# Holding back two groups of loads beside DMA transposes in the first phase of a fused attention and expert kernel

## The chip, the cores and the metric

The kernel runs on one core of one Trainium2 chip. The metric is the device time of one execution in microseconds (us); a lower time is better. The engines are named PE (matrix multiply; PEld in the tables is its loading of weights), DVE (vector), ACT (scalar), POOL (which here mostly issues loads) and SP (which here issues the DMA transposes). Times within a trace are counted from the start of the span, which reaches from the first to the last instruction.

## The reference, cut to what matters

Eight batches of linear attention with eight heads are computed, and their output goes through eight experts with a balanced (Sinkhorn) gate. Only the attention and the first expert matter here.

```python
def phi(x, c, s):                       # cos and sin weights of the position
    r = np.maximum(x, 0.0)
    return np.concatenate([r * c, r * s], axis=-1)
q_p = phi(q, cos_w, sin_w)
k_p = phi(k, cos_w, sin_w)
kv = np.einsum('bhsf,bhsd->bhfd', k_p, v)
z = np.sum(k_p, axis=2)
num = np.einsum('bhsf,bhfd->bhsd', q_p, kv)
den = np.einsum('bhsf,bhf->bhs', q_p, z)[..., None] + 1e-06
# num / den is x of the experts: out += P[:, e] * (relu(x @ w1[e]) @ w2[e])
```

## The kernel before

The first phase runs in blocks. Block j does the first expert on 512 tokens in 16 slots, eight of the first matrix product (`ffn1`, PSUM tile `h_ps`, result `hT`) and eight of the second (`ffn2`, `y_ps`). Between the slots stands the attention work of other batches: in block 1, the third batch (number 2 in the code) is finished and the fourth (number 3) is prepared. In the code, `hk` counts the four pairs of heads; `zsel` holds the sums of the scaled keys, `rb` the reciprocals of the denominators, and `xT` is x, the input of the experts. In the traces an instruction that waits holds up those written behind it on its engine: before the change the value copy at 55.41 us on DVE, whose v had landed by 43.19, ran only after a `q_p` that had waited 7.94 us.

Loads go through POOL's software queue into four buffers for each of q, k and v; a load takes half a batch. The scaled queries `q_p` of batch 2 and later are turned by a DMA transpose that SP issues; there are three `q_p` buffers, and one comes free when its transpose has landed (in the trace before, the first transpose landed at 53.97 us, and the `q_p` that waited for its buffer began at 54.07).

```python
ld = p1.enter_context(tc.tile_pool(name="ld", bufs=4))
qp_pool = p1.enter_context(tc.tile_pool(name="qp_pool", bufs=3))
rb_pool = p1.enter_context(tc.tile_pool(name="rb_pool", bufs=4))
# ...
def load(b, half, names="qkv", held_back=False):
    for name in names:
        x = ld.tile([P, 2, C, D], F16, name=f"{name}_ld")
        # ... i = nc.gpsimd.dma_start(out=x, in_=this half of the batch)
        if held_back:
            after(ve.last, i)          # wait for DVE's last instruction so far

def prep_q(b, hk):
    q16 = loaded.pop(("q", b, hk))
    # ... from batch 2 on: relu in place on DVE
    q_p = qp_pool.tile([P, C, 2, D], F16, name="q_p")
    ve.tensor_tensor(out=q_p[:], in0=q16.unsqueeze(2).to_broadcast([P, C, 2, D]),
                     in1=cs, op=ALU.mult)
    # ... from batch 2 on:
    nc.sync.dma_start(out=qTs[b, hk], in_=q_p[:].rearrange("p c a d -> p (c a d)"),
                      transpose=True)
```

The schedule of block 1 (j = 1, b = 2), cut:

```python
# the third batch (b): its scaled keys and values, sums, denominators, x
for hk in range(HK):
    if hk >= 2:
        at(j, 0, prep_k, b, hk, False)
    at(j, 0, prep_kp, b, hk)
    at(j, (0, 0, 1, 3)[hk], prep_v, b, hk, (ve.tensor_copy, se.copy)[hk // 2])
at(j, 3, sums, b, 0)                 # PE; afterwards zsel on DVE
at(j, 5, sums, b, 1)
at(j, 6, denominators, b)            # PE needs zsel and the four transposed q
for hk in range(HK):
    at(j, (9, 10, 12, 13)[hk], attend, b, hk)      # PE, then xT on DVE
# the fourth batch (b + 1)
    (4, prep_q, 0), (5, prep_q, 1), (6, prep_k, 0), (7, prep_q, 2),
    (8, prep_k, 1), (9, prep_q, 3), (10, prep_kv, 0), (10, prep_k, 2),
    (12, prep_kv, 1), (12, prep_k, 3), (13, prep_kv, 2), (14, prep_kv, 3),
# block 2 begins on the fifth batch with (3, prep_k, 0) on ACT
```

The softmax here doesn't subtract the row's maximum and nothing guards it: scores larger than these inputs give would overflow.

## Time and profile before

| | before |
|---|---|
| median of the first 3 runs | 989.77 us (989.68 to 989.98) |
| PE busy over the span | 969.5 of 988.3 us |
| PE idle in one piece, 48.97 to 55.91 us | 6.94 us |
| PE's clock at half | 53.96 to 60.79 us |

The page's own lines on busy time (first) and on the chain of work that ended last (second) say that PE bounds the kernel, so a microsecond that counts is one in which PE stands or runs slower.

```profile
PE 969.5 (98%) x7877; PEld 676.3 (68%) x7877; DVE 807.0 (82%) x1833; ACT 565.3 (57%) x1263; POOL 60.6 (6%) x82
...
PE 93%; DVE 2%; ACT 2%; DMA 2%; POOL 0%; issue 0%; ACTq 0%; SPq 0%; DVEq 0%; POOLq 0%
```

The table of 10 us stretches shows, for each, PE's busy time (with the number of its instructions), the same of the other engines, then PE's clock, the DMA share and GB/s. One row differs from the rest.

```profile
core 0: us, PE busy (x) PEld busy (x) DVE busy (x) ACT busy (x) POOL busy (x), PEclk, DMA share, GB/s
40.00:50.00 10.00, 8.97 (x53) 4.06 (x51) 5.37 (x13) 7.93 (x18) 0.86 (x2) 1.00 1.20 201
50.00:60.00 10.00, 3.74 (x42) 2.02 (x43) 5.83 (x13) 1.13 (x4) 0.00 (x0) 0.70 0.83 132
60.00:70.00 10.00, 10.00 (x123) 5.00 (x122) 7.19 (x17) 6.21 (x16) 0.00 (x0) 0.96 0.51 86
```

PE's timeline about the hole. In square brackets stand the idle time before the instruction and what ended it.

```profile
45.32 3.66 PE L109 MATMUL h_ps<-xT,w1e 128*128 128x512 f16 x16
55.91 0.68 PE L109 MATMUL small_ps<-acc_lo,k_p 64*128 64x65 f16 x18 [6.94 <-DVE acc_lo L109]
56.94 0.68 PE L109 MATMUL small_ps<-acc_lo,k_p 64*128 64x65 f16 x18 [0.35 <-DVE acc_lo L109]
57.55 3.48 PE L109 MATMUL h_ps<-xT,w1e 128*128 128x512 f16 x8
60.96 0.75 PE L109 MATMUL small_ps<-acc_lo,k_p 64*128 64x65 f16 x36
```

PE waits 6.94 us for `acc_lo`, which is where the third batch's value copies lie. The line at 57.55 shows the second loss: eight matmuls of 512 columns take 3.48 us. DVE's timeline says why the copies are late.

```profile
45.83 0.30 DVE L109 TENSOR_SCALAR q_ld<-q_ld 128x576 f16<-128x576 f16 x1
54.07 0.76 DVE L109 TENSOR_TENSOR q_p<-q_ld,acc_hi 128x1152 f16<-128x1152 f16 x1 [7.94 <-DMA q_pT<-q_p]
54.74 0.75 DVE L109 TENSOR_TENSOR k_p<-k_ld,acc_hi 128x1152 f16<-128x1152 f16 x1
55.41 0.44 DVE L109 COPY acc_lo<-v_ld 128x576 f16<-128x576 f16 x1
```

DVE has a `q_p` to write and no buffer for it until the first transpose has landed. In the chain of waits, that transpose is one piece.

```profile
39.69 14.29 DMA q_pT<-q_p
...
54.07 0.76 DVE q_p L109
```

The transpose takes 14.29 us from issue to landing; transposes that are issued alone later land after 3.2 to 3.6 us. What stands beside it is in POOL's timeline: the six loads of the fourth batch, issued as soon as buffers are free. (The last line shown is the first load of the fifth batch.)

```profile
33.86 0.72 POOL L201 DMA_DIRECT2D k_ld<-in_k_dram  x1 [0.61 <-DMA w2e<-in_moe_w_dram]
...
40.84 0.72 POOL L201 DMA_DIRECT2D v_ld<-in_v_dram  x1 [0.70 <-ACT rb L109]
71.58 0.72 POOL L201 DMA_DIRECT2D q_ld<-in_q_dram  x1 [30.02 <-DVE acc_lo L109]
```

In the trace these six land between 45.16 and 53.96 us, one each 1.3 to 2 us.

### The profile page before, as it was taken

To read this page: it belongs to the slowest core of one execution; us is meant where nothing else is said; L and a number is where in the kernel's file an instruction comes from. 1 tells how busy PE (TensorE), PEld (TensorE's weight loads), DVE (VectorE), ACT (ScalarE), POOL (GpSimd) and SP (SyncE) were. 2 spreads that over 40 slices of the span, in tenths; PEclk is the share of its full clock that TensorE was granted. 3 is DMA by queue.
4 is the path that set the end of the run, shared out by engine and by line. 5 is a ranking of instruction groups with operands and counts; after the bars stand their busy time and mean duration, and the time that the engine had idled before them with its cause. 6 is when DMAs were issued, how large, how long until landed. Compare 5 with 4: busy or idle time off the path is not lost.

```text
span 988.3 us, 20283 instructions
## 1 busy us (share of the span) xinstructions
PE 969.5 (98%) x7877; PEld 676.3 (68%) x7877; DVE 807.0 (82%) x1833; ACT 565.3 (57%) x1263; POOL 60.6 (6%) x82
## 2 busy tenths in 40 slices
PE   9979999989999999999999999999999999999997
PEld 6535544447777777777777777777777777777775
DVE  6666774779889888988789888988789888988887
ACT  5746665467776555555555555555555555555551
POOL 6312110010000000000000000000000000000001
PEclk9989999999999999999999999999999999999999
DMA  9968991633013310133113410133103400104535
GB/s 162 204 111 147 162 148 31 126 62 73 26 48 68 69 47 25 34 83 68 41 33 67 85 31 26 49 67 68 49 25 67 92 25 26 48 26 113 132 86 128
DMA packets 80336, 73.54 MB, mean 74 GB/s; under 512 B 33264, under 2 KB 72176, under 8 KB 80240
## 3 DMA queue, kind: packets, MB, share of 16 engines
q0 software_dynamic: 27232, 30.94, 20.0%
q1 hardware_dynamic: 52768, 41.06, 16.9%
q8 instruction: 61, 1.00, 0.4%
q14 instruction: 35, 0.29, 0.1%
q10 hardware_dynamic: 240, 0.26, 0.1%
HBM read 83.12 MB, written 12.98 MB: 97 GB/s over the span
## 4 chain that ended last, share of the span: by engine, by line
PE 93%; DVE 2%; ACT 2%; DMA 2%; POOL 0%; issue 0%; ACTq 0%; SPq 0%; DVEq 0%; POOLq 0%
PE rows_ps L109 34%; PE h_ps L109 27%; PE copied_ps L109 11%; PE p_ps L109 11%; PE y_ps L109 6%; PE small_ps L109 4%; DMA q_pT<-q_p 1%; ACT hT L109 0%; DVE acc_hi L913 0%; POOL hs_last L928 0%; DVE P_tok L109 0%; DMA out_dram<-acc_lo 0%; DVE colp L109 0%; ACT u L109 0%; ACT acc_lo L109 0%
## 5 line engine op out<-in xcount | busy, mean ns | idle before, releaser
L913 DVE SCALAR_TENSOR_TENSOR acc_lo<-rows_ps,P_tok,acc_lo 128x512 f32<-128x512 f32 (+1 forms) x322 | 203.5, 641 | 74.7 <-PE rows_ps L109 74.6
L109 PEld LDWEIGHTS <-H 128*128 128x128 f16 x2080 | 203.0, 98 | 83.1 <-issue 1.2
L849 ACT CAST u<-h_ps 128x384 f16<-128x384 f32 x288 | 137.8, 478 | 131.2 <-PE h_ps L109 131.2
L109 PEld LDWEIGHTS <-w1e 128*128 128x128 f16 x1632 | 156.8, 98 | 67.5 <-issue 8.0
L843 DVE CUSTOM_DVE_ANT_0 H<-p_ps,u 128x384 f16<-128x384 f32 x329 | 181.4, 551 | 6.5 <-PE p_ps L109 6.4
L109 PEld LDWEIGHTS <-hs 128*128 128x128 f16 x1500 | 146.6, 98 | 56.2
L109 PE MATMUL h_ps<-S,w1e 128*128 128x384 f16 x672 | 164.1, 326 | 1.1 <-ACT u L109 0.9
L109 PE MATMUL p_ps<-xT,T 128*128 128x384 f16 x672 | 164.1, 326 | 0.1
L109 PE MATMUL h_ps<-xT,w1e 128*128 128x384 f16 (+1 forms) x616 | 151.6, 354 | 0.2 <-DVE xT L109 0.2
L109 PE MATMUL rows_ps<-V,H 128*128 128x256 f16 x1000 | 150.0, 273 | 0.7 <-DVE acc_hi L913 0.7
L109 PE MATMUL rows_ps<-w2e,hs 128*128 128x256 f16 x1000 | 150.0, 273 | 0.0
L881 ACT ACTIVATE H<-h_ps 128x384 f16<-128x384 f32 x144 | 70.7, 491 | 95.0 <-PE h_ps L109 95.0
L109 PEld LDWEIGHTS <-T 128*128 128x128 f16 x1008 | 98.1, 98 | 29.2 <-issue 2.8
L109 PE MATMUL rows_ps<-w2e,H 128*128 128x256 f16 (+1 forms) x568 | 91.2, 285 | 0.0
L862 ACT COPY copied_ps<-h_ps 128x384 f32<-128x384 f32 x144 | 67.5, 469 | 35.2 <-PE h_ps L109 35.2
L872 ACT ACTIVATE H<-copied_ps 128x384 f16<-128x384 f32 x144 | 70.9, 492 | 20.3 <-PE copied_ps L109 20.3
L109 PE MATMUL copied_ps<-xT,w1e 128*128 128x384 f16 x336 | 82.1, 326 | 0.0
L109 PE MATMUL h_ps<-S,T 128*128 128x384 f16 x336 | 81.8, 325 | 0.3 <-ACT copied_ps L109 0.3
L109 PE MATMUL copied_ps<-w2e,H 128*128 128x256 f16 x504 | 75.5, 272 | 0.0
L109 PE MATMUL rows_ps<-V,hs 128*128 128x256 f16 x500 | 75.0, 272 | 0.0
L913 DVE SCALAR_TENSOR_TENSOR acc_lo<-copied_ps,P_tok,acc_lo 128x256 f32<-128x256 f32 x126 | 60.2, 478 | 0.4
L913 DVE SCALAR_TENSOR_TENSOR acc_hi<-rows_ps,P_tok,acc_hi 128x512 f32<-128x512 f32 (+1 forms) x56 | 41.3, 738 | 20.5 <-PE rows_ps L109 19.7
(147 smaller groups left out, 953.5 us busy)
## 6 DMA issues: line engine op xcount, KB each, us to landing
S<-x_saved SPq DMA_DIRECT2D x108, 192.0 KB, 2.4
out_dram<-acc_lo SPq DMA_DIRECT2D x62, 128.0 KB, 2.4
w1e<-in_moe_w_dram POOLq DMA_DIRECT2D x7, 1024.0 KB, 9.0
w2e<-in_moe_w_dram POOLq DMA_DIRECT2D x7, 1024.0 KB, 9.7
q_ld<-in_q_dram POOLq DMA_DIRECT2D x16, 288.0 KB, 7.4
k_ld<-in_k_dram POOLq DMA_DIRECT2D x16, 288.0 KB, 8.2
v_ld<-in_v_dram POOLq DMA_DIRECT2D x16, 288.0 KB, 9.6
x_saved<-S SPq DMA_DIRECT2D x18, 192.0 KB, 1.9
```

What stands on the lines that cost most here:

```text
L109: i = getattr(self.engine, name)(*args, **kwargs)
L843: latest = ve._custom_dve(TENSOR_ADD_SAT, out=out, in0=ps[:, 0:TU], in1=t[:], s0=FP32_MAX, s1=0.0)
L849: se.copy(out=t[:], in_=ps[:, 0:TU])
L862: se.copy(out=Y[:, 0:TU], in_=X[:, 0:TU])
L872: se.activation(out=h11, in_=Y[:, 0:TU], func=AF.Relu)
L881: se.activation(out=h12, in_=X[:, 0:TU], func=AF.Relu)
L913: ve.scalar_tensor_tensor(out=a, in0=rows, scalar=P_tok[:, g, self.e : self.e + 1], in1=a, op0=ALU.mult, op1=ALU.add,)
```

## The change

The intent is to let the third batch's transposes pass before the fourth batch's loads, and then the fourth batch's transposes before the fifth batch's loads. Nothing else moves: set against each other, the two kernels have the same instructions in the same order on PE, DVE, ACT and SP. On POOL the fourth batch's loads also change their order from k, k, q, q, v, v to q, k, v for each half.

```diff
@@ block 1, after the third batch's second prep_v @@
+                        if hk == 1:
+                            for half in range(2):
+                                at(j, 0, load, b + 1, half, "qkv", True)
@@ the loads of the batch after next @@
-            if j == 0:
+            if j and b + 2 < B:
                 for half in range(2):
-                    at(1, 0, load, b + 2, half)
-            elif b + 2 < B:
-                for half in range(2):
-                    at(j, 11 + half, load, b + 2, half, "qkv", True)
+                    at(j, (14 if j == 1 else 11) + half, load, b + 2, half, "qkv", True)
```

## The prediction

> **What bounds the kernel.** The page gives PE 969.5 of 988.3 us (98%); the chain that ended last is 93% PE. The change touches only the first 100 us. There the table of 10 us windows shows one hole: PE is busy 3.74 of 10 us in 50-60, mean clock 0.70. The timeline shows PE idle 6.94 us before 55.91, waiting for the third batch's value copies on DVE; DVE sat idle 7.94 us before 54.07, until a DMA transpose q_pT<-q_p landed (it frees one of three q_p buffers). The chain of waits holds it as one DMA item of 14.29 us from 39.69; transposes issued later, alone, land in 3.2 to 3.5 us. Reason: six loads of the fourth batch are issued at 33.9 to 40.8, and the software queue moves about 205 GB/s; the last lands at 53.96. From 44 to 51 both queues get the same packet rate. [...] After the hole PE runs at half clock: eight 512-column matmuls take 3.48 us, elsewhere about 1.73. The hole costs 6.9 + about 1 (second copy) + 1.7, about 9.6 us.
>
> **What the change does.** PE, DVE, ACT and SP instructions and their order are the same; 12 loads on POOL move. The fourth batch's six now wait for the copy of the third batch's second values (about 49.1 us) instead of free buffers, and go q,k,v per half. The fifth batch's wait for DVE's last value copy (76.2 before) instead of 71.3. No bytes change.
>
> **Gain.** The first transpose no longer competes: estimate, landing near 46 instead of 54. The copies are then ready at 48 and 49, just when PE needs them (49.0). Hole and half clock vanish: -9.6 us.
>
> **Given back (estimates from the trace's landing times).** With a quiet queue six loads issued from t land at t+4.4, +6, +7.5, +9, +10.5, +12.
> 1. The fourth batch's first q, issued at 49.4, lands near 53.8. DVE, in order, has its relu and q_p before the third batch's second zsel, which PE wants in slot 6 at 53.5: PE waits about 1.7 us.
> 2. The fourth batch's transposes (from 55) now collide with these loads, which end near 61.5; the last q_p needs the first transpose's buffer near 61.4 and gets it near 63. The x products behind it on DVE come late: about 1.5 us of PE in slots 12 and 13.
> 3. The fifth batch's first k lands about 6 us after 70.8, near 77; ACT wants it in slot 3 of block 2, near 74.5. ACT is blocked with two h_ps buffers: about 1.5 us of PE; the second half's k another 0.5.
> Together about 5 of the 9.6 us. [...] After block 2 all only shifts.
>
> **Prediction.** 985.2 us, 8 in 10 within 982.3 to 988.0. Chances: faster by over 2% 0.01, within 2% 0.98, slower by over 2% 0.01.
>
> **What would show it.** The DVE wait for q_pT<-q_p shrinks from 7.9 to under 3 us and moves to about 61; clock 1.0 through 50-60; a new DVE wait for q_ld of 2 to 4 us near 50-54; PE gaps near 54 (behind zsel), 63 (behind xT) and 77 (behind hT); ACT waits for k_ld in block 2; phases after 100 us of equal length.
>
> **What would make it wrong.** If the transposes at 55 to 62 suffer like the one at 39.69, the hole returns smaller in block 1: 988 or more. If the late loads land a little earlier than counted, slack hides items 2 and 3: 981 to 983.

Its landing times for a quiet queue are estimates from the trace before, where six loads issued from 112.35 us landed 4.39, 6.77, 8.18, 9.61, 11.10 and 12.50 us after that, and six issued from 131.99 us 4.75, 6.17, 7.65, 9.08, 10.51 and 12.14 us after that.

## The result, and the profile after

| | before | after |
|---|---|---|
| median | 989.88 us (989.68 to 990.12, 4 runs) | 987.47 us (986.80 to 988.09, 4 runs) |
| ratio to before | | 0.9976, 95% interval 0.9958 to 0.9993 |

A ratio is the mean time of one kernel's runs over that of the other's runs of the same rounds, so it is not quite the ratio of the medians. The gain is 2.4 us by the medians, where the hole and its half clock had cost about 9.6 us by the prediction's count. The question is where the rest went. To see it, the span is cut at four PE instructions that both kernels have. A is the first matmul of block 1, B the first of the third batch's `attend` (slot 9 of block 1), C the first of block 2, D the first of block 3. The columns are differences of their start times.

| us | up to A | A to B | B to C | C to D | D to the end | span |
|---|---|---|---|---|---|---|
| before | 45.32 | 21.22 | 8.84 | 19.65 | 893.25 | 988.28 |
| after | 45.68 | 13.01 | 11.56 | 22.83 | 893.30 | 986.38 |
| difference | +0.36 | -8.21 | +2.72 | +3.18 | +0.05 | -1.90 |

So 8.2 us were won in the first part of block 1, and 5.9 us were given back, in the rest of block 1 and in block 2. From block 3 on nothing changed. The stretches of the profile after:

```profile
40.00:50.00 10.00, 10.00 (x94) 4.93 (x91) 8.80 (x20) 7.93 (x19) 0.35 (x1) 1.00 0.86 146
50.00:60.00 10.00, 9.01 (x116) 4.40 (x115) 6.93 (x17) 6.44 (x15) 3.93 (x6) 1.00 1.02 157
60.00:70.00 10.00, 7.80 (x70) 3.90 (x69) 7.03 (x17) 4.76 (x11) 0.00 (x0) 1.00 0.86 143
70.00:80.00 10.00, 7.81 (x123) 4.21 (x116) 6.28 (x15) 4.91 (x12) 4.28 (x6) 1.00 0.77 115
80.00:90.00 10.00, 9.24 (x58) 4.44 (x57) 6.94 (x15) 6.91 (x17) 0.00 (x0) 1.00 1.22 174
```

The hole in 50-60 and its clock of 0.70 are gone, but PE's busy time is now short by 2.2 us in 60-70 and again in 70-80. PE's timeline after names the waits; the second line answers to the one at 55.91 before.

```profile
45.68 3.66 PE L109 MATMUL h_ps<-xT,w1e 128*128 128x512 f16 x16
49.27 0.74 PE L109 MATMUL small_ps<-acc_lo,k_p 64*128 64x65 f16 x36
49.95 1.90 PE L109 MATMUL h_ps<-xT,w1e 128*128 128x512 f16 x8
51.78 0.75 PE L109 MATMUL small_ps<-acc_lo,k_p 64*128 64x65 f16 x36
...
55.16 0.56 PE L109 MATMUL small_ps<-q_pT,zsel 128*32 128x192 f16 x12 [0.72 <-DVE zsel L109]
...
65.52 0.54 PE L109 MATMUL small_ps<-q_pT,kv_sb 128*64 128x384 f16 x4 [2.06 <-DVE xT L109]
...
79.84 1.02 PE L109 MATMUL h_ps<-xT,w1e 128*128 128x512 f16 x4 [2.19 <-ACT hT L109]
```

The sums now start at 49.27 without a wait, and the eight matmuls after them take 1.90 us. Three new gaps stand further on: 0.72 us behind `zsel`, 2.06 us behind `xT` and 2.19 us behind `hT`. DVE's timeline explains the first two.

```profile
48.90 0.45 DVE L109 COPY acc_lo<-v_ld 128x576 f16<-128x576 f16 x1
...
53.87 0.31 DVE L109 TENSOR_SCALAR q_ld<-q_ld 128x576 f16<-128x576 f16 x1 [2.23 <-DMA q_ld<-in_q_dram]
...
64.24 0.76 DVE L109 TENSOR_TENSOR q_p<-q_ld,acc_hi 128x1152 f16<-128x1152 f16 x1 [2.97 <-DMA q_pT<-q_p]
```

The copy at 48.90 is what releases the fourth batch's loads, and the copy at 70.85 the fifth batch's, as POOL's timeline shows.

```profile
49.65 0.72 POOL L201 DMA_DIRECT2D q_ld<-in_q_dram  x1 [16.73 <-DVE k_ld L109]
...
71.60 0.72 POOL L201 DMA_DIRECT2D q_ld<-in_q_dram  x1 [17.67 <-DVE zsel L109]
```

(The view names a later DVE instruction in both; by the edit it is the copy before it, which ended 0.30 us before the issue both times.) DVE then needs the first of them, q, at 51.64 and gets it at 53.87. At 61.27 it needs a `q_p` buffer again: the very wait of before, 7.94 us then and 2.97 us now, one batch later. ACT's timeline explains the third gap: ACT waits 3.32 us for the fifth batch's first k, with PE's two `h_ps` tiles behind it.

```profile
74.70 0.60 ACT L109 ACTIVATE hT<-h_ps 128x512 f16<-128x512 f32 x1 [0.27 <-PE h_ps L109]
78.62 0.68 ACT L109 ACTIVATE k_ld<-k_ld 128x576 f16<-128x576 f16 x1 [3.32 <-DMA k_ld<-in_k_dram]
```

In the chain of waits after, the first transpose of before is no longer a piece. Two others are.

```profile
72.31 6.23 DMA k_ld<-in_k_dram
...
79.04 7.80 DMA q_pT<-q_p
```

Landings in the two traces, from issue to landing (third batch: number 2):

| | before | after |
|---|---|---|
| third batch's first transpose | 39.69 to 53.97 | 40.05 to 44.20 |
| fourth batch's loads, first issue to last landing | 33.86 to 53.96 | 49.65 to 63.39 |
| fourth batch's first transpose | 60.27 to 63.48 | 55.06 to 64.15 |
| fifth batch's loads, first issue; first k landed | 71.58; 78.60 | 71.60; 78.54 |

The last row is telling: PE is about 5 us further on at that point than before (C is at 70.25, before at 75.38), yet the fifth batch's loads start at the same time as before, since they now wait for DVE's last value copy.

### The profile page after: what moved, and what is told of

Read it like the earlier page. It is cut to its first block, busy times and chain, and to the rows that moved or that the text cites. A ratio compares the mean times of both kernels' runs of the same rounds, so it can differ in the third digit from the quotient of the medians.

```text
span 986.4 us, 20281 instructions
## 1 busy us (share of the span) xinstructions
PE 968.7 (98%) x7877; PEld 676.4 (69%) x7877; DVE 806.8 (82%) x1833; ACT 565.6 (57%) x1263; POOL 60.6 (6%) x82
## 4 chain that ended last, share of the span: by engine, by line
PE 91%; issue 2%; ACT 2%; DVE 2%; DMA 2%; POOL 1%; ACTq 0%; DVEq 0%; POOLq 0%; SPq 0%
PE rows_ps L109 34%; PE h_ps L109 27%; PE copied_ps L109 11%; PE p_ps L109 11%; PE y_ps L109 5%; PE small_ps L109 3%; DMA q_pT<-q_p 1%; DMA k_ld<-in_k_dram 1%; ACT hT L109 0%; DVE acc_hi L913 0%; POOL hs_last L928 0%; DVE P_tok L109 0%; DMA out_dram<-acc_lo 0%; DVE colp L109 0%; ACT u L109 0%
## 5 line engine op out<-in xcount | busy, mean ns | idle before, releaser
L881 ACT ACTIVATE H<-h_ps 128x384 f16<-128x384 f32 x144 | 70.8, 491 | 95.0 <-PE h_ps L109 95.0
```

The source lines that it names most:

```text
L881: se.activation(out=h12, in_=X[:, 0:TU], func=AF.Relu)
```

## The experiments

The theory at this point: the gain is the hole with its half clock; it is given back at three places, of which the collision of the fourth batch's transposes with its own loads, felt through the `q_p` buffers, and the late loads of the fifth batch are the large ones. The main rival was the change's own intent: that the fifth batch has to wait for slots 14 and 15, because its loads would else hit the fourth batch's transposes. A second rival was that PE's hole had to do with the loaded data and not with the `q_p` buffer. Twelve runs were made (one of them the change itself, and one a repeat of e1), all with correct results, five or six runs each. Their times, beside the kernel before of the same rounds:

| run | what differs | median us (range) | before, median us | ratio (95% interval) |
|---|---|---|---|---|
| e1_hold4_only | first half of the change alone | 986.18 (983.75 to 986.47) | 990.01 | 0.9957 (0.9944 to 0.9969) |
| e2_hold5_only | second half alone | 991.55 (990.26 to 994.57) | 990.01 | 1.0020 (1.0009 to 1.0032) |
| e3_four_qp | before, four q_p buffers | 986.73 (985.98 to 987.22) | 990.01 | 0.9967 (0.9955 to 0.9979) |
| e4_q_free | change, the fourth batch's q not held | 986.85 (986.57 to 988.12) | 990.01 | 0.9972 (0.9961 to 0.9984) |
| e5_hold4_four_qp | first half, four q_p | 986.29 (982.52 to 989.89) | 989.82 | 0.9966 (0.9943 to 0.9989) |
| e6_order | as e5, two q_p later in DVE's order | 982.52 (981.99 to 985.08) | 989.82 | 0.9934 (0.9921 to 0.9947) |
| e7_rb3_only | before, three rb buffers (control) | 990.36 (989.45 to 990.65) | 989.82 | 1.0005 (0.9993 to 1.0017) |
| e8_change_four_qp | the change, four q_p | 984.18 (983.95 to 986.99) | 989.82 | 0.9954 (0.9942 to 0.9965) |
| e9_slot12 | as e5, fifth batch at slots 12, 13 | 982.69 (982.33 to 983.03) | 989.85 | 0.9927 (0.9914 to 0.9941) |
| e10_order_slot12 | e6 and e9, k ahead of q | 982.59 (982.39 to 984.39) | 989.85 | 0.9931 (0.9919 to 0.9944) |
| e11_change_again | the change | 987.69 (987.24 to 988.50) | 989.85 | 0.9980 (0.9967 to 0.9992) |
| e12_hold4_again | first half alone | 985.80 (984.80 to 986.17) | 989.85 | 0.9958 (0.9945 to 0.9970) |

The same cuts A to D for their profiles (one execution each):

| us | A to B | B to C | C to D |
|---|---|---|---|
| before | 21.22 | 8.84 | 19.65 |
| change | 13.01 | 11.56 | 22.83 |
| e11_change_again | 13.85 | 10.95 | 22.39 |
| e1_hold4_only | 13.02 | 13.50 | 19.65 |
| e12_hold4_again | 12.99 | 13.51 | 19.64 |
| e2_hold5_only | 20.49 | 8.85 | 21.56 |
| e3_four_qp | 18.40 | 8.84 | 19.64 |
| e4_q_free | 13.43 | 12.71 | 20.81 |
| e5_hold4_four_qp | 12.96 | 9.42 | 26.72 |
| e8_change_four_qp | 13.54 | 8.84 | 21.30 |
| e9_slot12 | 13.18 | 9.72 | 19.64 |

D to the end is between 893.2 and 893.9 us in all of them.

### The halves of the change: e1_hold4_only, e2_hold5_only, e11_change_again, e12_hold4_again

```diff
 # e1 and e12: against the change
-at(j, (14 if j == 1 else 11) + half, load, b + 2, half, "qkv", True)
+at(j, 11 + half, load, b + 2, half, "qkv", True)
 # e2: against the kernel before
-at(j, 11 + half, load, b + 2, half, "qkv", True)
+at(j, (14 if j == 1 else 11) + half, load, b + 2, half, "qkv", True)
```

> Only the first half of the change: the fourth batch's loads are held, the fifth batch's stay at slots 11 and 12. Theory (holding the fifth batch to slots 14 and 15 is a cost, because its first k lands 3.3 us after ACT wants it): its loads are issued near 67.1 us instead of 71.6, the first k lands near 73 and the ACT wait for k_ld in block 2 and the PE wait behind hT (2.2 us) are gone; the time is 984.5 to 985.5 us, 2 to 3 us under the change. Rival (the later slots are needed, because earlier loads collide with the third and fourth batches' transposes): a new DVE or PE wait for q_pT of 2 us or more, and 987 us or more.

> Only the second half: the fourth batch's loads as before, the fifth batch's held to slots 14 and 15. Theory: the hole of 7 us before 56 us and the half clock after it stay as before; the fifth batch's first k lands near 83 us where ACT wants it at 80.3, PE waits 1 to 2.5 us behind hT in block 2: 991 to 992.5 us. Rival (later loads help the transposes): 989.9 us or less.

> The change itself again, to compare it in the same rounds with the next one. Theory: 987 to 988 us; gaps of PE behind zsel (0.7), xT (2.1) and hT (2.2) as in its first profile.

> Only the first half of the change again (the fifth batch's loads at slots 11 and 12). Theory: 1 to 2.5 us under the whole change of the same rounds, since the wait for k_ld in block 2 is not there; 985.5 to 986.5 us. Rival (the difference of 1.3 us seen between separate jobs is noise): within 0.5 us of the whole change.

The first half alone gave 985.80 us in the rounds in which the whole change gave 987.69, so the second half cost 1.9 us. Alone on the kernel before, it cost 1.5 us by the medians, and its interval excludes 1. In e1 and e12, C to D is back at 19.65 us: the waits for k_ld and hT in block 2 are gone, because the fifth batch's loads were issued at 66.6 us instead of 71.6. In e2 that part is 1.9 us longer, and the hole stays (6.56 us). The theory's mechanism held; with three `q_p` buffers, the rival's collision did not occur. One time and one gap did not come as expected: e1's 986.18 us is over its 984.5 to 985.5, and in e11 the gap behind `zsel` was 1.56 us and not 0.7.

But e1's gain was smaller than C to D alone would give, since B to C became 1.9 us longer than with the change, although its gap behind `xT` was about the same. The row for 60-70 us of e12 shows the reason: the clock.

```profile
60.00:70.00 10.00, 7.43 (x36) 3.31 (x36) 6.59 (x17) 4.11 (x10) 3.27 (x5) 0.83 0.95 161
```

The gap of 2.50 us before 65.19 was followed by a lower clock: the mean of the row is 0.83, and eight matmuls of 512 columns from 67.67 took 3.06 us, against 1.90 from 67.75 after the change. In e1 the mean over 60 to 70 us was 0.83 too, after a gap of 2.22 us, and the eight took 2.90 us. The single runs fit this: the one run of e1 with a mean clock of 1.000 took 983.75 us, the four with 0.998 took 985.78 to 986.47. In both profiles of the change the gap there was 2.06 and 1.76 us, and the clock stayed whole. The last section comes back to this.

### The buffer: e3_four_qp and its control e7_rb3_only

```diff
-qp_pool = p1.enter_context(tc.tile_pool(name="qp_pool", bufs=3))
+qp_pool = p1.enter_context(tc.tile_pool(name="qp_pool", bufs=4))      # e3
-rb_pool = p1.enter_context(tc.tile_pool(name="rb_pool", bufs=4))
+rb_pool = p1.enter_context(tc.tile_pool(name="rb_pool", bufs=3))      # e3 and e7
```

> The kernel before with four q_p buffers instead of three (and three rb buffers instead of four[...]); no load is moved. Theory (loads delay the transposes, and PE feels it through the q_p buffer that the first transpose holds): the transposes still land late (first near 54 us, 14 us after its issue), but DVE no longer waits 7.9 us for it; the copies are ready at 49 us and the hole before slot 4 is gone. PE then waits in slot 6 (wanted at 53.5) for the last of the four transposes, near 57.5: 4 us. Time 984 to 986 us. Rival (PE waits for the loaded data or for DVE itself, not for the buffer): the hole stays and 989.9 us.

> Control: the kernel before with three rb buffers instead of four, nothing else. Theory: no effect, 989.5 to 990.3 us, the same hole of about 7 us. If it is faster by 1 us or more, part of what the runs with four q_p buffers gained is from this and not from them.

(In e3 the `rb` pool gives up one buffer; e7 tests that part alone.) In e3 the first transpose was as late as before, 38.82 to 53.72 us, and yet the hole in slot 4 was gone. PE met the four transposes one by one in slot 6 instead:

```profile
53.76 0.35 PE L109 MATMUL small_ps<-q_pT,zsel 128*32 128x192 f16 x6 [1.04 <-DMA q_pT<-q_p]
55.47 0.50 PE L109 MATMUL small_ps<-q_pT,zsel 128*32 128x192 f16 x6 [1.36 <-DMA q_pT<-q_p]
56.47 0.51 PE L109 MATMUL small_ps<-q_pT,zsel 128*32 128x192 f16 x6 [0.50 <-DMA q_pT<-q_p]
57.81 0.51 PE L109 MATMUL small_ps<-q_pT,zsel 128*32 128x192 f16 x6 [0.83 <-DMA q_pT<-q_p]
```

These waits are 3.73 us together, against 4 expected, but the time, 986.73, lies over the 984 to 986 expected: PE also ran in part at a lower clock (mean 0.78 over 50 to 60 us and 0.88 over 60 to 70), which the expectation had left out. The control is within noise of before (interval 0.9993 to 1.0017). So having only three `q_p` buffers made PE feel the late transpose as early and as long as it did. That the loads make it late is shown by the change, e1 and e12, not by e3. The second rival is refuted.

### The fourth batch's q not held: e4_q_free

```diff
+                    for half in range(2):
+                        at(j, 0, load, b + 1, half, "q")          # free, as before
 # and after the second prep_v:
-                                at(j, 0, load, b + 1, half, "qkv", True)
+                                at(j, 0, load, b + 1, half, "kv", True)
```

> The change, but the fourth batch's two q loads go free as before and only its k and v loads are held. Theory: two loads more delay the first transpose by about 2.5 us (landing near 46.7 instead of 44.2), DVE and PE lose 0.5 us before slot 4; DVE's 2.2 us wait for q_ld near 54 and the one for the second q go; with four loads instead of six in the way the fourth batch's first transpose lands near 60 instead of 64.2 and DVE's 3 us wait for it shrinks under 1 us, with it PE's 2.1 us behind xT. The waits for k_ld in block 2 stay. Time 984 to 985.5 us. Rival (all loads must be held to free the transposes): the first transpose lands after 50 and 987 us or more.

Half of it came: the third batch's first transpose landed at 47.55 us, DVE waited 1.95 us for it and PE 0.94 and 0.57 us for the copies, and the waits for q_ld were gone. The other half failed. The fourth batch's first transpose landed at 63.50, not near 60, and PE's gap behind `xT` was 2.11 us as before. The later copy released the four loads only at 51.0, and these four still took until 62.69 to land. PE also ran in part at a lower clock (mean 0.83 over 60 to 70 us). At 986.85 us it gained little over the change, and the expected 984 to 985.5 was missed.

### Four q_p buffers with the hold: e5_hold4_four_qp, e8_change_four_qp, e9_slot12

e5 is e1, and e8 the change, each with e3's two buffer edits. e9 is e5 with this:

```diff
-at(j, 11 + half, load, b + 2, half, "qkv", True)
+at(j, (12 if j == 1 else 11) + half, load, b + 2, half, "qkv", True)
```

> The fourth batch's loads held as in the change, the fifth batch's at slots 11 and 12 as before, and four q_p buffers (three rb buffers). Theory (what is left of the collision in block 1 reaches PE through the q_p buffer): the fourth batch's first transpose still lands 9 us or so after its issue, but DVE no longer waits 3 us for it before the last q_p; PE's gap of 2.2 us behind xT near 63 and the half clock after it go. Time 982 to 983.5 us. Rival (DVE is late there for other reasons, as the late q or k loads): the gap stays, 985 to 986.5 us.

> The whole change with four q_p buffers (three rb buffers). Theory: the gap behind xT near 63 (2.1 us) goes, the gap behind hT in block 2 (2.2 us) stays at 1.5 to 3 us, since the fifth batch's loads are still issued only after DVE's last value copy: 984.5 to 986 us, and 2 us or more above the same kernel with the fifth batch's loads at slots 11 and 12. Rival (the two waits are one and the same delay, so that removing the first removes the second): within 1 us of that kernel.

> The run with four q_p buffers and only the fourth batch held was split: three times 982.5 to 984.0, three times 988.6 to 989.9 us; in its profile the fifth batch's loads, issued at 64.0 us (slot 11), went ahead of the last transpose of the fourth batch, issued at 64.9, which then took 13.3 us, and PE waited 5.5 us for it in block 2. Here the fifth batch's loads are held one slot more, to slots 12 and 13; nothing else differs. Theory (the order of those two, within 1 us, splits it): no run over 985 us, all 982 to 984.5; the loads are issued near 66 us, after the transpose, which lands in 3.2 to 4 us. Rival (the split has another cause): runs of both kinds remain.

In e5 and e8 the DVE wait for the buffer and the gap behind `xT` of 2 us went, as expected (B to C 9.42 and 8.84 us). e8's gap behind `hT` stayed, 1.61 us with ACT waiting 2.74 us for k_ld, so the two waits are not one. The times alone would not say so: e8's 984.18 us is only 0.9 above the median of the three shorter runs of e5 (described next), where 2 or more were expected and the rival had said within 1; it is 1.5 above e9, which ran in other rounds.

e5 brought a surprise: three of its six runs took 982.52 to 983.96 us, the other three 988.62 to 989.89. The profile is of the longer kind, and its PE timeline and chain of waits show what happened in block 2.

```profile
78.23 0.51 PE L109 MATMUL small_ps<-acc_hi,zsel 128*32 128x192 f16 x6 [5.47 <-DMA acc_hi<-q_p]
```

```profile
64.89 13.30 DMA acc_hi<-q_p
```

With the fourth buffer DVE no longer stood still, so that it released the fifth batch's loads at slot 11 (issued from 64.02) just before SP issued the fourth batch's last transpose (64.89). That transpose then took 13.30 us, and PE waited 5.47 us for it: the hole of before, in block 2. So the main rival, that the fifth batch's loads would hit the fourth batch's transposes, was right after all, in a kernel in which DVE is not delayed. The wait for the transpose in e1 had by chance kept the loads behind it.

e9 tests this by one slot: the loads were issued from 66.06 us, after the transpose (64.09), which landed in 3.31 us. All five runs lie within 982.33 to 983.03 us. No profile of a shorter run of e5 was taken, so that the order of those two decided its two kinds of runs is shown by e9 and by the longer profile, not by a pair of e5's profiles.

### The order on DVE: e6_order, e10_order_slot12

```diff
-(4, prep_q, 0), (5, prep_q, 1), (6, prep_k, 0), (7, prep_q, 2),
+(5, prep_q, 0), (6, prep_k, 0), (7, prep_q, 1), (7, prep_q, 2),    # e6, e10
 # e10 also: e9's edit, with "kqv" instead of "qkv" in block 1
```

> As the run before it, and the fourth batch's first q_p is made after the third batch's second zsel, its second q_p after the denominators. Theory: PE's gap of 0.7 us behind zsel near 54 goes, since DVE no longer waits for the q load ahead of it; 0.5 to 1 us less than the run before it, 981.5 to 983 us. Rival: the work moved only makes PE wait later, for hl or xT: no less than the run before it.

> All together: fourth batch held as in the change, four q_p buffers, the fourth batch's first two q_p moved behind zsel and the denominators, the fifth batch's loads at slots 12 and 13 with k ahead of q. Theory: the transposes go first and the k that ACT wants near 72 us lands near 70.5; no PE gap over 1 us is left before 100 us; 981 to 982.5 us, all runs within 1.5 us of each other, 7.5 to 9 us under the kernel before.

The gap behind `zsel` went in both, but others came: 0.48 us for rb and 0.78 (e6) or 1.77 us (e10) behind `xT`, since DVE had more to do before the first `xT`. e6's 982.52 us lies 0.7 under the median of e5's three shorter runs, but the ranges overlap and e5's two kinds of runs spoil the comparison, so neither forecast is decided; in e6's profile the last transpose was issued 0.27 us before the loads and took 6.52 us. In e10 the k landed at 72.40, not 70.5, the spread was 2 us and not 1.5, a PE gap over 1 us remained, and the time, 982.59 us, is just over the expected 981 to 982.5 and equals e9's. So the order is worth nothing that these runs can show.

The best version is e9, by its narrow range (e6 and e10 have the same median within 0.2 us): 982.69 us, 7.2 us under the kernel before by the medians and 5.0 under the change of the same rounds. It is still within 2% of both.

## Why the prediction was right or wrong

- **The hole and its cause: right.** DVE waited for a `q_p` buffer, the transpose for the loads. e3 showed the buffer's part, the change the loads' part (first landing 4.15 us after issue instead of 14.29).
- **The gain: right.** A to B was to become 7.9 us shorter (9.6 less 1.7 for the wait behind `zsel`) and became 8.2 shorter in the first profile and 7.4 in the second. The clock stayed whole in 50-60, as said. By the start times of PE's lines, 9.54 us were won up to the second sums in both profiles (60.96 less 45.32 before, 51.78 less 45.68 after), against 9.6 predicted. The denominators then gave back 0.95 and 1.79 us against 1.7 (as gaps behind `zsel`, 0.72 and 1.56 us; half of their matmuls ran before the gap, and in the second profile q landed 0.65 us later), and 0.4 us more went behind `hl`, which the prediction did not have.
- **The collision in block 1: right in kind, too small.** Predicted 1.5 us, measured 2.7 (first profile) and 2.1 us (second). The term behind it is the landing of the fourth batch's first transpose: predicted 63, measured 64.15. So DVE waited 2.97 us for the buffer and not about 1.6 (61.4 to 63). The prediction let the six loads end near 61.5, as with a quiet queue, but in the mix with the transposes they ended at 63.39.
- **The fifth batch's loads: right in kind, too small.** Predicted 2.0 us, measured 3.2 and 2.7. The loads were issued at 71.60 and not at 70.8, because DVE came later out of the wait above, and the first k landed 6.9 us after the first issue, against 6 reckoned. ACT waited 3.32 us for the first k and 1.08 us for the second half's, and the collision of block 1 repeated itself in block 2 between the fifth batch's own transposes and loads (first transpose 7.80 us), with 0.76 us of PE behind `xT`, which the prediction had left out.
- **The sum.** -9.6 + 1.7 + 1.5 + 2.0 was to be -4.4 (the text rounds to 985.2, that is -4.6); measured -2.4. The step that failed is the size of two terms, 1.2 us too small each in the first profile, and they hang together: one late transpose makes DVE late, and DVE releases the next loads.
- **No term for the clock in what is given back: right for the two profiles of the change, but not safe.** In both the mean clock was 1.000. In e1, e4 and e12, gaps of 2.22, 2.11 and 2.50 us at the same place were followed by a lower clock (mean 0.83 over 60 to 70 us in all three). Two of the change's four first runs show a mean clock of 0.998 instead of 1.000; where in them is not known.
- **"After block 2 all only shifts": right,** 893.25 and 893.30 us.

## What to carry to other kernels

A DMA that an engine was soon to wait for landed 14.29 us after its issue beside a queue of loads that nobody needed yet, and 4.15 us after it with these loads held. So try to hold such loads until the urgent DMAs are through, and no longer, since their own first consumers soon wait (ACT 3.32 us for the fifth batch's first k). When a wait goes through a shared chain, here DVE's order, its removal moves what the same engine releases: the wait for a `q_p` buffer, 7.94 us before, came back one batch later with 2.97 us. So look for the next collision one round later. And if a buffer count decides how early a late transfer is felt, one buffer more can be worth as much as the reordering: the hold of the fourth batch and a fourth buffer, with the fifth batch one slot later, gave 7.2 us (e9), where the buffer alone gave 3.3 (e3) and that hold alone 4.1 (e12).

## What the traces show of the clock, the transposes and the loads

- A lower clock followed some of PE's gaps and not others. With the gap of 6.94 us before the change the clock was at half from 53.96 to 60.79 us. After gaps of 2.22 us (e1), 2.11 (e4) and 2.50 (e12) the mean clock over 60 to 70 us was 0.83. In e3 the four gaps of 1.04, 1.36, 0.50 and 0.83 us before 57.81 went with a mean clock of 0.78 over 50 to 60 us and 0.88 over 60 to 70. In the profile of the change the clock stayed at 1.00 with gaps of 2.06 and 2.19 us; in the profiled runs of e11 and e8, whose longest gaps there were 1.96 and 1.61 us, the mean clock was 1.000. The gap of 2.11 us was followed by a lower clock and the one of 2.19 us was not, so the length of one gap alone does not tell these apart; what does is not shown here.
- A transpose next to loads cost time: it landed after 3.2 to 3.6 us alone (the four issued from 60.27 to 69.68 before the change), after 13.3 to 14.9 us beside a queue of loads (before, e3, e5), after 9.1 us with five loads still out (after the change, issued at 55.06).
- From 44 to 51 us before the change the queues of the loads and of the transposes moved 1032 and 1033 packets, 147 to 148 per us each (as the trace counts them). Equal packets are not equal bytes: a load is 256 packets of 1152 bytes, a transpose, of the same 288 KB, is 1152 packets of 256 bytes (12288 for the 48 loads and 27648 for the 24 transposes in the trace before). At that rate the packets of one transpose alone would take 7.8 us, an estimate from these counts. Besides, the transpose issued at 39.69 had its first packet only at 43.67, with eight loads still out, the one issued at 55.06 after the change at 59.10, with five out; the one issued at 40.05 after the change, with two loads out, had it after 1.3 us, and the one issued at 60.27 before the change, alone, after 1.2 us. What sets these delays is not shown.
- Loads issued early were not free here: those issued from 33.9 us on, whose data DVE first wanted at 51.6 (by the trace after), were what made the hole of 7 us.
